# Batch 0's v in four-token runs, w_in in two halves, and slots 0 to 8 in a written order

## The chip, the cores and the metric

The kernel runs on one core of a Trainium2 chip. The metric is the device time of one execution in microseconds (us), from the runtime's own clock; the median of three runs is given, and beside it one execution taken with the hardware profiler. The core's engines are TensorE (PE, matrix multiplies; PEld is its weight load), VectorE (DVE), ScalarE (ACT), GpSimd (POOL) and SyncE (SP). Each works through its own list of instructions in order and waits on semaphores for the others. DMAs are asked for on three of these lists: SP's, ACT's and POOL's.

## The reference

Two stages in one kernel: sliding-window attention with ALiBi bias, then a two-matrix feed-forward block with a hard-swish.

```python
# q, k, v: (8 batches, 8 heads, 576 tokens, 64), float32
scores = scale * q @ k^T                       # scale = 1/8
bias   = slope[h] * -|i - j|,  slope[h] = 2^-(h+1)
mask   = 0 <= i - j < 128                      # causal, window of 128 tokens
attn   = softmax(where(mask, scores + bias, -1e9))
x      = (attn @ v) as 4608 tokens x 512       # heads side by side
h      = x @ w_in                              # w_in: 512 x 2048
out    = (h * clip(h + 3, 0, 6) / 6) @ w_out   # w_out: 2048 x 512, out float32
```

## The kernel before, in words

A **slot** g is one batch and one pair of heads: g = 4 * batch + pair, 32 slots in all. For each slot q and k have to stand with the 64 head dimensions on partitions (`qTb`, `kTb`), the scores are made in PSUM, ScalarE takes the exponential into `pd` (the diagonal 128x128 blocks) and `po` (the blocks below), and the values are multiplied with `v`, to which a column of ones is appended (`vbuf`, 65 wide), so that the row sums come out beside the values. They are divided (`avs`), transposed back, and copied into `xT`, a ring of four batches with d_model on partitions.

The feed-forward part works on blocks nt of 512 tokens. `moe_up(nt, ms)` is one of 16 steps, four 128x512 matmuls with `w_in_sb` into a PSUM bank, then one ACT instruction (`r`, L520) and one DVE instruction (`gbuf`, L521). `moe_down(nt, step)` is four matmuls with `w_out_sb` (L551) of one of four row blocks of 128 tokens; after four of them the bank is copied (L560) and sent out. The list `units` holds all of these steps in order, and `fill(n)` puts the next n of them behind whatever was just issued. So attention's latencies are to be covered with feed-forward steps.

The order is written by hand (`manual_schedule` for all five engines): `first_batch()`, `second_batch()`, then `segment()` for slots 8 to 31. What matters for the change:

- **Batch 0.** q and k come with nine consecutive tokens in each partition (`load_run`), are cast (`prepare`, L208), transposed on TensorE in 64x64 pieces (`transposes`, L219) and copied to `qTb`/`kTb` (L220). For batches 0 and 1 the bias and the mask of the off blocks, for batch 0 also that of the diagonal blocks, are added by TensorE from a table (`tables_diag` L271, `tables_off` L307/L310). v comes token by token (`load_tokens`, L112): each of 128 partitions is one token and receives one 256-byte piece per head, five DMAs for a batch.
- **Slots share space.** `pd` and `po` of slots 0 to 3 lie in `w_out_sb` (`rooms`), those of slots 4 to 7 in `gbuf[1]`. So w_out cannot be loaded before batch 0's values are done. PSUM has two big tiles (`ps_sc`, two banks each, for scores, wide transposes and batch values) and four single banks (two "h", one "av", one "o").
- **Weights.** w_in is loaded on POOL's list with a cast to bf16 in four quarters of 512 columns (`load_w_in`, L166), so that a quarter serves four of the 16 up-steps; the asks stand between POOL's casts. w_out comes in four quarters of 512 rows (`load_w_out`, L171), all asked for in `second_batch` behind slot 6.
- **Later batches.** q and k of batches 1 and 2 come with `load_double` (L98), are cast on POOL (`prepare_double`, L227), transposed (`wide_double` L254, nine 128x128 transposes; `double` L242 in parts of five and four) and copied. From batch 3 on they are transposed by DMA. Slots 8 and up mask their blocks on POOL after the exponential (L405, L414).

## Time and profile before

| what | us |
|---|---|
| median of three runs (322.14 to 323.13) | 322.87 |
| the profiled execution, its own time | 323.39 |
| its span, first to last instruction | 321.4 |
| PE busy, share of the span | 309.9, 96% |
| ACT busy | 195.8, 61% |
| DVE busy | 173.6, 54% |
| POOL busy | 140.2, 44% |
| first up-step on PE starts | 21.3 |
| last w_in quarter landed | 40.5 |
| first down-step on PE starts | 53.8 |
| last w_out quarter landed | 59.8 |

All times inside the execution count from the span's start. "Busy" of PE counts a matmul from its start to its modelled end, and matmuls overlap, so the busy share hides the small pauses; the start times of neighbouring matmuls show them. The granted TensorE clock is 1.0 from beginning to end (0.99 in the last 22 us).

### The profile page before, as it was taken

Reading aid. Unit: us, or ns where it says so; the run is one execution under the profiler, and the core shown is the slowest. Engines: PE = TensorE matmul, PEld = TensorE weight load, DVE = VectorE, ACT = ScalarE, POOL = GpSimd, SP = SyncE. Lnnn points to the kernel's source line nnn. Section 1 sums busy time; section 2 is a strip of 40 time slices with the busy share of each in tenths; the row PEclk is TensorE's granted clock in tenths of the full one; section 3 lists DMA queues with packets and bytes.
Section 4 is the critical chain, followed back from the end, with each engine's and each line's share of the span. In section 5 each row is a group of like instructions: output and inputs, shape, how many; then the busy total and the mean of one; then the engine's idle time right before and its main releaser. Section 6 shows DMA issues by size and latency. Waiting matters only on the chain.

```text
span 321.4 us, 7126 instructions
## 1 busy us (share of the span) xinstructions
PE 309.9 (96%) x2776; PEld 164.8 (51%) x2776; DVE 173.6 (54%) x338; ACT 195.8 (61%) x334; POOL 140.2 (44%) x249
## 2 busy tenths in 40 slices
PE   7879898999999999999999999999999999999996
PEld 6555455454554454444677654444444444444443
DVE  6757565664445555655565546554655455455510
ACT  4748876877777766766676667666764344244401
POOL 7455295586393866276645662763331000000000
PEclk9999999999999999999999999999999999999999
DMA  7999999999999999999999999942212200000112
GB/s 269 205 319 200 233 274 185 234 241 210 201 248 169 217 198 217 196 222 216 208 202 203 228 182 191 246 78 86 23 55 66 73 34 35 33 33 35 65 53 77
DMA packets 131425, 51.90 MB, mean 161 GB/s; under 512 B 118976, under 2 KB 123328, under 8 KB 131392
## 3 DMA queue, kind: packets, MB, share of 16 engines
q1 hardware_dynamic: 126160, 45.36, 66.4%
q0 software_dynamic: 4224, 4.19, 8.4%
q10 hardware_dynamic: 1008, 1.90, 1.6%
q8 instruction: 21, 0.34, 0.5%
q14 instruction: 12, 0.10, 0.1%
HBM read 36.70 MB, written 9.44 MB: 144 GB/s over the span
## 4 chain that ended last, share of the span: by engine, by line
PE 84%; DMA 7%; SPq 3%; POOL 2%; ACT 1%; issue 1%; DVE 1%; ACTq 0%; POOLq 0%
PE ops L551 38%; PE hps L501 36%; DMA ldbuf<-in_q_dram 3%; PE sce L364 3%; PE av L441 2%; DMA w_in_sb<-in_moe_w_in_dram 2%; SPq L112 2%; PE av L433 2%; DMA ldbuf<-in_k_dram 2%; SPq L98 1%; PE ops L532 1%; POOL w_out_sb L171 1%; PE tp L242 1%; POOL pr L227 1%; ACT r L520 0%
## 5 line engine op out<-in xcount | busy, mean ns | idle before, releaser
L521 DVE SCALAR_TENSOR_TENSOR gbuf<-r,hps 128x512 bf16<-128x512 f32 x144 | 98.8, 687 | 102.2 <-ACT r L520 100.9
L520 ACT ACTIVATE r<-hps,bias 128x512 f32<-128x512 f32 x144 | 98.9, 689 | 88.6 <-PE hps L501 88.3
L501 PE MATMUL hps<-xT,w_in_sb 128*128 128x512 bf16 (+1 forms) x640 | 144.9, 358 | 1.7 <-DMA w_in_sb<-in_moe_w_in_dram 1.5
L551 PE MATMUL ops<-w_out_sb,gbuf 128*128 128x512 bf16 x560 | 137.9, 380 | 0.0
L501 PEld LDWEIGHTS <-w_in_sb 128*128 128x128 bf16 x640 | 59.1, 98 | 56.7 <-DMA w_in_sb<-in_moe_w_in_dram 2.3
L551 PEld LDWEIGHTS <-gbuf 128*128 128x128 bf16 x560 | 51.8, 98 | 56.4
L414 POOL TENSOR_SCALAR_AFFINE_SELECT po<-po 128x512 bf16<-128x512 bf16 x48 | 30.2, 633 | 32.7 <-ACT po L412 32.5
L405 POOL TENSOR_SCALAR_AFFINE_SELECT pd<-pd 128x512 bf16<-128x512 bf16 x48 | 29.6, 631 | 31.6 <-ACT pd L388 31.6
L388 ACT ACTIVATE pd<-sce,bias_d 128x512 bf16<-128x512 f32 x48 | 31.6, 683 | 5.4 <-PE sce L372 5.4
L194 POOL CAST tbuf<-ldbuf 128x512 bf16<-128x512 f32 (+1 forms) x45 | 25.5, 611 | 18.6 <-DMA qTb<-tbuf 9.4
L560 DVE COPY osb<-ops 128x512 f32<-128x512 f32 x33 | 22.7, 688 | 20.0 <-PE ops L551 19.9
L412 ACT ACTIVATE po<-sce,bias_o 128x512 bf16<-128x512 f32 x48 | 32.9, 686 | 0.0
L452 DVE TENSOR_TENSOR avs<-av,rc 128x384 bf16<-128x384 f32 (+1 forms) x48 | 23.6, 491 | 1.6
L441 PEld LDWEIGHTS <-pd 128*128 128x128 bf16 x192 | 14.3, 97 | 8.3 <-POOL tbuf L194 0.5
L433 PE MATMUL av<-vbuf,po 128*128 128x65 bf16 x192 | 18.0, 193 | 0.0
L441 PE MATMUL av<-vbuf,pd 128*128 128x65 bf16 x192 | 17.3, 194 | 0.3 <-ACT kTb L244 0.3
L187 POOL CAST vbuf<-ldbuf 128x1024 bf16<-128x1024 f32 x14 | 14.2, 1041 | 5.4 <-DMA ldbuf<-in_v_dram 5.4
L433 PEld LDWEIGHTS <-po 128*128 128x128 bf16 x192 | 14.3, 98 | 2.9 <-DVE avs L452 0.5
L227 POOL CAST pr<-ldbuf 128x576 bf16<-128x576 f32 x20 | 12.8, 668 | 6.0 <-DMA ldbuf<-in_k_dram 3.8
L417 ACT ACTIVATE p4buf<-sce,bias_d 128x64 bf16<-128x64 f32 x48 | 15.4, 321 | 0.0
L364 PE MATMUL sce<-qTb,kTb 64*64 64x192 bf16 (+1 forms) x368 | 11.9, 246 | 0.0
L364 PEld LDWEIGHTS <-kTb 64*64 64x64 bf16 x368 | 7.1, 106 | 8.6 <-issue 8.5
(104 smaller groups left out, 207.8 us busy)
## 6 DMA issues: line engine op xcount, KB each, us to landing
out_dram<-osb SPq DMA_DIRECT2D x33, 256.0 KB, 2.4
ldbuf<-in_v_dram SPq DMA_DIRECT2D x32, 256.0 KB, 5.1
ldbuf<-in_q_dram SPq DMA_DIRECT2D x20, 256.0 KB, 4.8
ldbuf<-in_k_dram SPq DMA_DIRECT2D x16, 256.0 KB, 4.5
ldbuf<-in_q_dram SPq DMA_DIRECT2D x12, 288.0 KB, 7.5
ldbuf<-in_k_dram SPq DMA_DIRECT2D x12, 288.0 KB, 7.8
w_in_sb<-in_moe_w_in_dram POOLq DMA_DIRECT2D x4, 512.0 KB, 9.6
w_out_sb<-in_moe_w_out_dram POOLq DMA_DIRECT2D x4, 512.0 KB, 10.2
```

What stands on the lines that cost most here:

```text
L194: nc.gpsimd.tensor_copy(out=tbuf[:m, :, j, :], in_=s[:m, j, :, :].rearrange("p (i e) d -> p i (e d)", e=2))
L364: nc.tensor.matmul(sce[e][lo:lo + 64, j, :, :].rearrange("p s c -> p (s c)")[:, ds(lo, n)], lhsT=kT[r, j, lo:lo + 64], rhs=qT[r, ds(128 * ...
L388: nc.scalar.activation(out=pd[:, e, :, :], in_=st["sce"][e][:, :, 0, :], func=ACT.Exp, bias=bias_d[:, h:h + 1], scale=scale)
L405: nc.gpsimd.affine_select(out=pd[:, e, :, :], in_=pd[:, e, :, :], pattern=[[0, 4], [1, 128]], channel_multiplier=-1, base=0, compare_op=AL ...
L412: nc.scalar.activation(out=po[:, e, :, :], in_=sc[:, :, 1, :], func=ACT.Exp, bias=bias_o[:, h:h + 1], scale=scale)
L414: nc.gpsimd.affine_select(out=po[:, e, :, :], in_=po[:, e, :, :], pattern=[[0, 4], [-1, 128]], channel_multiplier=1, base=-1, compare_op=A ...
L433: nc.tensor.matmul(out_av, lhsT=po[:, e, qt % 4 if full(g) else qt - 1, :], rhs=vb[:, qt - 1, h, :], start=True, stop=False)
L441: nc.tensor.matmul(out_av, lhsT=d, rhs=vb[:, qt, h, :], start=(qt == 0), stop=True)
L501: nc.tensor.matmul(hps[:, lo:hi], lhsT=w_in_sb[:, ks, ts(ms, 128)], rhs=xT[:, ks, ds(src, hi - lo)], start=(ks == 0), stop=(ks == n_ks - 1))
L520: nc.scalar.activation(out=r6, in_=hps, func=ACT.Relu, bias=bias3[:, 0:1], scale=1.0 / 6.0)
L521: nc.vector.scalar_tensor_tensor(out=gts[nt][:, ms, :], in0=r6, scalar=1.0, in1=hps, op0=ALU.min, op1=ALU.mult)
L551: nc.tensor.matmul(ops[nt, sub], lhsT=gts[nt][:, ms, ts(sub, 128)], rhs=w_out_sb[:, ms, :], start=(ms == 0), stop=(ms == n_ms - 1))
```

## The change

The functions `first_batch` and `second_batch`, with `prepare` and `transposes`, go. In their place a text, `PLAN`, lists one step per line, and `run_plan` calls a function for each; the functions do what the old ones did, cut into single pieces, so that casts, transposes, copies, scores, exponentials, masks, values, and up- and down-steps can stand in any order. `segment` now begins at slot 20 instead of 8. From the scores of slot 13 on, TensorE's instructions follow in the same order as before.

- **v of batch 0** is loaded as four-token runs: partition p of 128 holds tokens 4p to 4p+3 of four heads, in pieces of 1024 bytes (`ldv`, two DMAs), and the last 64 tokens as before (`ldl`). Two casts (`cr`) put them into `tbuf`. TensorE then sorts them (`vp`, `unshuffle`): a 0/1 matrix `sel`, made on VectorE (`sel`: a memset, a reduce, a copy), picks for each block j of 128 tokens the rows 32j to 32j+31, once for each of the four tokens t, summed in PSUM. That is 16 matmuls with 32 rows and 512 columns, two blocks side by side in two banks, and four copies to `vbuf` (`ve`).
- **w_in** comes in two halves of 1024 columns (`wp 0`, `wp 1`) on POOL's list. Both stand behind the casts of batch 1's first k and q.
- **w_out**'s four quarters (`wout`) stand on POOL's list behind the casts of batch 2's q and k of the first double pair.
- **Order.** Batch 0's values are formed in pieces (`vf`, `vr`, `vl`) into a part of `gbuf[0]` (`avs0`). Scores of slots 5 and 4 and all four transposes of batch 1 (`dt 1 ...`) stand ahead of the first up-step, which is now step 6 (`u 0 6`). The up-steps then run in a mixed order: 6, 0, 4, 3, 5, 7, 14, 2, 9, 12, 13, 11, 1, 15, 8, 10.
- **Slots 8 and 9** use the split scores (diagonal and off tiles apart) as slots 4 to 7 do, without tables, with the masks on POOL (`QF = 10`). `p4buf` has four instead of two.
- Some casts and copies change engine: five of batch 2's and 3's k and q casts go from POOL to ACT, two of batch 1's to DVE; one of batch 0's transposed q goes from DVE to ACT.

Counted over the whole program: 16 matmuls with `sel` more, 3 warm-up matmuls fewer (27 for 30), 4 score matmuls fewer net; POOL 9 casts and 2 DMA asks fewer.

```diff
-    def second_w_in():
-        nc.gpsimd.memset(w_out_sb[:, 4, 0:1], 0.0)
-        load_w_in(1)
...
     def scores(g):
-        if full(g):
+        if g < QF:
             scores_diag(g)
             scores_off(g)
             return
...
+    def s_sel():
+        nc.vector.memset(sel, 0.0)
+        diag = sel.rearrange("p (t c) -> p t c", t=4)[:, :, 0:128:4]
+        nc.vector.tensor_reduce(out=diag[:, 0, :], in_=ident.rearrange("p (j i) -> p i j", j=4),
+                                op=ALU.max, axis=mybir.AxisListType.X)
+        nc.vector.tensor_copy(out=diag[:, 1:4, :],
+                              in_=diag[:, 0:1, :].to_broadcast([128, 3, 32]))
...
+    def s_ldv(b, h, n):
+        nc.sync.dma_start(out=vsource(b)[0][:, ds(h, n), :],
+                          in_=v[b, ds(h, n), 0:512, :].rearrange("h (p t) d -> p h (t d)", t=4))
...
+    def s_cr(b, h, n, eng):
+        C[eng](out=vruns[:, :, ds(h, n), :].rearrange("p t h d -> p h t d"),
+               in_=vsource(b)[0][:, ds(h, n), :].rearrange("p h (t d) -> p h t d", t=4))
+
+    def unshuffle(b, h, n, j0, banks):
+        for t in range(4):
+            for i, ps in enumerate(banks):
+                r = slice(32 * (j0 + i), 32 * (j0 + i) + 32)
+                nc.tensor.matmul(ps, lhsT=SEL[r, t, 0:128], rhs=vruns[r, t, ds(h, n), :],
+                                 start=(t == 0), stop=(t == 3))
...
+    def s_wp(i, k0, n):
+        nc.gpsimd.dma_start(out=w_in_sb[:, ds(k0, n), ts(i, 1024)],
+                            in_=moe_w_in[ds(k0 * 128, n * 128), ts(i, 1024)].rearrange(
+                                "(k p) f -> p k f", p=128))
...
-    def first_batch():
-        prepare(0, (V, A))
-        warm_up(20)
...
-    def second_batch():
...
+    def run_plan(text):
+        for line in text.split("\n"):
+            if line.strip():
+                name, *args = line.split()
+                STEPS[name](*(int(a) if a.isdigit() else a for a in args))
...
-        load_tokens(0, "v")
         constants()
         memsets()
-        memsets_later()
-        first_batch()
-        second_batch()
-        fill(2)
-        segment(2 * NP, G, lambda g: FILLS.get(g, (1, 1, 1, 2, 0, 1, 2)))
+        run_plan(PLAN)
+        done[0] = 20 - 1
+        segment(20, G, lambda g: FILLS.get(g, (1, 1, 1, 2, 0, 1, 2)))
```

The plan's first part, up to the first down-step; each step is a line of its own in the kernel and is separated by a semicolon here. V, A and P name the engine of a copy (DVE, ACT, POOL); h, av, o and sc name PSUM banks. `c0` casts a run of batch 0, `t0` transposes it, `e0` copies it out; `td`/`sd` and `to`/`so` are tables and scores of the diagonal and off tiles; `xt`, `xd`, `xo` the exponentials, `md` a mask; `ldd`, `ldt` loads of q or k and of tokens; `pd`, `dt`, `de` cast, transposes and copy of a double pair; `vf`, `vr`, `vl`, `at` values and `nf`, `nr`, `nl`, `na` their division; `bf`, `br`, `bk` transposes back and `ef`, `er`, `ek` copies to `xT`; `vt` casts v; `u`, `ur`, `um` an up-step's PE, ACT and DVE parts, `ub` a begun one; `d` a down-step.

```
c0 1 k A; wu 20; sel; td 0; to 0; c0 0 k V; ldv 0 0 4; mem 7; c0 1 q P; wu 7; c0 0 q V; t0 0 q h; t0 0 k o; t0 1 k h; mem 3;
ldv 0 4 4; t0 1 q av; e0 0 k A; e0 0 q V; sd 0; xt 0; so 0; ldt 1 v 4; td 1; ldd 1 0 q 0; e0 1 q V; e0 1 k A; sd 1; c0 2 k P;
xo 0; ldl 0; xt 1; t0 2 k av; c0 3 k P; t0 3 k h; c0 2 q V; td 2; cr 0 0 4 P; ldd 1 0 k 0; t0 2 q h; e0 2 q A; to 2; e0 2 k V;
sd 2; so 2; pd 1 0 q 0 P; e0 3 k V; mem 6; ldd 1 0 k 1; cr 0 4 4 V; vp 0 0 h av; ve 0 0 8 0 1 V; ve 0 0 8 1 1 V; c0 3 q A;
t0 3 q h; pd 1 0 k 0 P; ldd 1 0 q 1; xt 2; xo 2; e0 3 q V; gl 2 0 P; to 1; so 1; xo 1; vp 0 2 h av; ve 0 0 8 2 1 A; td 3; sd 3;
cl 0 V; to 3; xt 3; so 3; xo 3; pd 1 0 q 1 P; vf 2 h; wp 0 0 4; pd 1 0 k 1 V; dt 1 0 k 0 9 sc; nf 2; ldt 1 v 2; ve 0 0 8 3 1 V;
dt 1 0 q 0 9 sc; de 1 0 k 0 9 A; mem 2; de 1 0 q 0 9 V; ldd 1 1 q 1; vl 3; vf 1 o; vr 0 2 4 h; sd 5; nl 3; xd 5 1; to 5; nf 1;
ldd 1 1 k 1; nr 0 2 4; wp 1 0 4; vr 0 3 3 av; nr 0 3 3; vr 2 2 4 h; nr 2 2 4; ldd 1 1 q 0; pd 1 1 q 0 P; pd 1 1 q 1 P; so 5;
xd 5 0; xo 5; vf 0 h; nf 0; md 5 0; vt 1 4; mem 4; bf 1 av; sd 4; xd 4 1; ef 1 0 512 V; ldd 1 1 k 0; pd 1 1 k 0 V; ldd 2 1 k 0;
ldt 1 v 1; xd 4 0; to 4; so 4; xo 4; bf 3 h; ef 3 0 256 V; pd 1 1 k 1 P; br o; bf 2 h; ef 3 256 256 A; bf 0 av; md 5 1; ldt 1 v 3;
dt 1 1 q 0 9 sc; ef 2 0 512 V; ef 0 0 512 A; de 1 1 q 0 9 V; mem 1; dt 1 1 k 0 9 sc; de 1 1 k 0 9 V; u 0 6 av; ur 0 6; um 0 6;
md 4 1; u 0 0 h; ur 0 0; um 0 0; er A; u 0 4 h; md 4 0; sd 6; xd 6 1; ur 0 4; um 0 4; xd 6 0; ldt 1 v 0; sd 7; u 0 3 o; xd 7 0;
u 0 5 h; xd 7 1; ur 0 5; um 0 5; u 0 7 av; ldt 2 v 3; ur 0 7; um 0 7; ldd 2 0 k 0; ur 0 3; to 7; to 6; um 0 3; vt 1 2; vt 1 0;
mem 0; u 0 14 h; ur 0 14; ldd 2 0 q 1; um 0 14; ldd 2 1 q 0; u 0 2 h; ur 0 2; so 7; xo 7; ldd 2 0 k 1; md 6 0; so 6; u 0 9 o;
ur 0 9; ldt 2 v 2; um 0 2; u 0 12 h; ur 0 12; ldt 3 q 0; u 0 13 av; md 7 1; um 0 9; xo 6; pd 2 0 k 0 P; at 5; md 6 1; ldd 2 0 q 0;
um 0 12; na 5; ldt 2 v 0; pd 2 1 q 0 P; pd 2 0 k 1 P; ldt 2 v 1; md 7 0; ur 0 13; um 0 13; u 0 11 h; at 4; ur 0 11; bk 5 o;
...
pd 2 0 q 0 P; pd 2 0 q 1 P; dt 2 0 q 0 9 sc; um 0 15; de 2 0 q 0 9 A; ek 6 V; ub 1 0 3 o; na 7; ldd 2 1 q 1; bk 7 sc; u 0 10 h;
pd 2 1 q 1 A; ek 7 V; u 1 4 h; u 1 0 o; ur 0 10; um 0 8; wout 1; um 0 10; ur 1 0; ur 1 4; dt 2 1 q 0 5 av; de 2 1 q 0 5 V; sd 8;
xd 8 0; sd 9; wout 0; vt 2 2; u 1 7 h; mem 5; xd 9 1; um 1 0; um 1 4; ur 1 7; u 1 6 av; um 1 7; xd 8 1; u 1 9 h; xd 9 0; ur 1 9;
ur 1 6; ct 3 q 0; vt 2 0; wout 2; um 1 9; u 1 2 o; wout 3; md 8 0; um 1 6; u 1 10 h; ur 1 10; um 1 10; so 8; so 9; ur 1 2; xf 8 1;
u 1 5 h; um 1 2; u 1 8 av; ldd 2 1 k 1; ur 1 8; xf 8 0; x4 8 0; x4 8 1; um 1 8; u 1 3 h; m4 8; ur 1 5; d 0 1 0 o; d 0 1 1 o; um 1 5;
pd 2 1 k 0 P; d 0 0 0 av; xf 9 0; mf 8 0; d 0 0 1 av; ldd 3 1 k 0; d 0 0 2 av; pd 2 1 k 1 A; ur 1 3; um 1 3; ldt 3 q 3; ...
```

## The prediction

> **What bounds the kernel now.** I read the stretches first, cut at two places. By 26.7 us TensorE has done as much useful work as the changed order puts ahead of its first up-step; at 91.1 us stand the last values of slot 11, and from the scores of slot 13 just behind them both orders are the same on TensorE.
>
> ```profile
> 0.00:26.70 26.70, 21.48 (x399) 15.39 (x400) 17.78 (x52) 14.89 (x19) 15.06 (x35) 1.00 1.02 262
> 26.70:91.10 64.40, 61.47 (x604) 32.59 (x601) 36.06 (x62) 51.08 (x86) 38.62 (x63) 1.00 1.08 222
> 91.10:321.40 230.30, 226.97 (x1778) 116.78 (x1777) 119.77 (x224) 129.86 (x230) 86.50 (x153) 1.00 0.66 133
> ```
>
> Behind the length stand PE, PEld, DVE, ACT, POOL, the granted clock and the DMA engines' share. In the last stretch TensorE is busy 227.0 of 230.3 us, some 3 of the rest being the last output: TensorE is the bound, and its list there is not changed. The change is worth what it does to the arrival at the second cut. Ahead of that cut the DMA engines never rest (1.02, 1.08). Next TensorE's waits, then its timeline:
>
> ```profile
> PE hps L501 <- DMA w_in_sb<-in_moe_w_in_dram: 1.5, 3, 0.8
> PE tp L242 <- POOL pr L227: 1.0, 1, 1.0
> PE tp L254 <- POOL pr L227: 0.9, 1, 0.9
> ```
> ```profile
> 28.80 1.04 PE L501 MATMUL hps<-xT,w_in_sb 128*128 128x512 bf16 x4 [0.49 <-DMA w_in_sb<-in_moe_w_in_dram]
> 35.83 1.04 PE L501 MATMUL hps<-xT,w_in_sb 128*128 128x512 bf16 x4 [0.81 <-DMA w_in_sb<-in_moe_w_in_dram]
> ...
> 49.05 0.45 PE L242 MATMUL tp<-ident,pr 128*128 128x128 bf16 x5 [1.00 <-POOL pr L227]
> ...
> 54.66 1.03 PE L501 MATMUL hps<-xT,w_in_sb 128*128 128x512 bf16 x4
> 55.52 0.44 PE L242 MATMUL tp<-ident,pr 128*128 128x128 bf16 x5
> ```
>
> The waits are short and many. The last two rows price an up-step: 55.52 - 54.66 = 0.86 us. The other engines' timelines show why the waits are there:
>
> ```profile
> 7.32 1.02 ACT L395 ACTIVATE w_out_sb<-scd 128x1024 bf16<-128x1024 f32 x1 [0.49 <-PE scd L296]
> 8.39 1.02 ACT L376 ACTIVATE w_out_sb<-sco 128x1024 bf16<-128x1024 f32 x1
> ```
> ```profile
> 28.52 1.48 POOL L166 DMA_DIRECT2D w_in_sb<-in_moe_w_in_dram  x2
> 43.55 2.99 POOL L171 DMA_DIRECT2D w_out_sb<-in_moe_w_out_dram  x4
> 47.70 2.50 POOL L227 CAST pr<-ldbuf 128x576 bf16<-128x576 f32 x4
> ```
>
> Batch 0 is a ping-pong of scores and exponentials; w_in's last two quarters are asked for at 28.5 us and landed at 35.8 and 40.5; the four w_out asks (2.99 us of POOL) hold up the casts that TensorE waits 1.00 us for at 49.05.
>
> **The work ahead of the first up-step, after.** TensorE, by differences of start times: four times 36 small transposes at 0.79 (3.2); 8 diagonal tables at 0.215 (1.7); six off tables at 0.44 (2.6); scores of six slots, a pair of 64-row matmuls in 0.055 (3.0); values of four slots at 0.53 (2.1); 20 transposes back and 36 of batch 1 at 0.055 (3.1); the unshuffle. Its 32-row matmuls are not in the trace. Bounds: alone, 16 x 0.215 = 3.4; two at a time, as the 64-row score pairs run, 1.7. I take 1.7, the row nearest in form: different rows of the array, different banks. Sum 17.4 us, the warm-up apart. Before, the same work less the unshuffle was done at 26.7 us.
>
> **When it is done (T).** ACT's list ahead of it: ten exponentials of 1024 at 0.92 from start to start (9.2), five copies or casts of 576 (2.8), four exponentials of 512 at 0.59 (2.4), one copy of 1152 (1.0), three smaller ones (1.4): 16.8. It starts with slot 1's k, landed at 6.3, so T is at least 23.1. In the batch 0 of before ACT worked 8.5 of 12.5 us; at that share T is 31.0. I go through the steps between. `sel` (three small DVE instructions, some 0.5) stands ahead of slot 0's casts, which begin at 5.2 and not 4.7; the first transposes start at 6.2 (before 5.4), slot 0's scores at 7.7 (6.9). Each further table needs one of two score tiles, released by an exponential. The unshuffle wants both v casts: the last q, k land at 9.6, then 1.0 MB in 1024-byte pieces, between 2.6 us (q, k rate, 0.74 per 288 KB) and 4.2 (v rate, 1.0 per 256 KB); I take 2.7, 1024 bytes being nearer to q's 2304 than to 256. So v is there at 12.3, the cast at 12.9, the two unshuffles at 13.2 and 15.6, each with its copies in front of the next scores. Last exponential of batch 0 ends 19.1; batch 1's first k copied 20.1; slot 3's values divided 21.9 (its tile is then slot 5's off table); slot 5's off exponential 24.1; slot 4's 26.6; copy of slot 0 into `xT` 27.4. T = 27.5, 0.8 later than before. DVE's list to there adds to 19.0 from 4.6, which makes 23.6: it is not the bound, but close.
>
> **w_in.** The ask waits for the cast of batch 1's q: behind v on SP's queue come two small loads (1.0) and four of 0.74, landed 16.3; cast 0.67; asked 17.0, where quarter one was asked for at 12.4. w_out's quarters landed 3.3 apart, so a half takes 6.6; about 3 us of loads on SP's queue run beside it: first half 27, just hidden. The second stands behind it on the same queue: 34. TensorE wants it for up-step 14, behind six up-steps (5.2), two score groups (0.5) and two tables (0.9): 34.1. I count 0.5 for it. On SP a load of batch 2's k waits for DVE's cast of batch 1's last k (26); queued behind it are three tiles of batch 1's v. I take it that they land by 36.5, behind w_in, and POOL's casts of them end at 37.7; the values of slot 5 want them at 39.1: 1.4 us of cover.
>
> **What goes and stays from T to the second cut.** 57.4 us of work took 64.4 before. Pauses over 0.15 us add to 4.4: two for w_in (1.6), the casts and the mask chain around 45 to 50 us (1.7), and four of 0.2 to 0.3 later. They go with the order; the other 2.6 are switches between matmul forms and stay. New pauses: between none and 4.4 again; I take 1.2, the 0.5 for w_in and 0.7 where an up-step waits for a bank (ACT's seven instructions between 30 and 35 us make it late with step 3, whose bank step 9 wants at 36.2).
>
> **At nothing:** w_out, asked for from 44.4 on, landed near 49, 52, 56 and 59 at 3.3 each, wanted from 57.5 to 61.8: cover 2 to 5 us, and without it 0.9 per step that waits. Slots 8 and 9 in split form (18 matmuls for 10 or 23, about 0.5 us each way). Five casts more on ACT (2.9) against five `xT` copies fewer (2.7), in a stretch where it is busy 51.1 of 64.4. SP's load for batch 3 that waits for a POOL cast near 58 holds batch 3's q and batch 2's last v tile, wanted at 68, landed 63.
>
> **Sum.** +0.8 (T) - 4.4 + 1.2 = -2.4 us. The profiled execution's own time is 323.39 (span 321.4 and 2.0 around it): 321.0. It lies 0.5 above the median of 322.87, so 320.5 for the median.
>
> **Rivals.** *The second half of w_in is late (slower).* For it: the last two quarters of before needed 12 us from ask to landing beside SP's loads; at that pace both halves need 24, land at 41.0, and TensorE stands 6.9 us at up-step 14 where I count 0.5: 326.9. It decides from a landing at 37.0 on (34.1 + 0.5 + 2.4), where the gain is gone. Against it: those 12 us were shared with v's 256-byte tiles, and w_out's quarters passed by such tiles:
>
> ```profile
> 50.26 10.56 SPq L112 DMA_DIRECT2D ldbuf<-in_v_dram  x5
> ```
>
> The first of these, asked for at 50.3, landed at 60.1, right behind the last of w_out at 59.8. The Trainium skill, "DMA: Bandwidth & Descriptors", section "Queues, rings and completion order", has each DMA engine take turns between queues packet by packet; by that rule w_in would share evenly with batch 2's q and k, whose pieces are nearly as long, and by an estimate from the 6.6 above, doubled for the second half, land near 40.2 and give 326.1. The v row agrees with turns by packet, since small pieces then get little; no row here has w_in beside q and k alone.
>
> *Nothing gained.* The unshuffle does not pair (+1.7) and the small pauses come back in part (+0.7): 322.9. For it: no 32-row row; two unshuffles on the chain. *All gained.* ACT waits half as long as I walked (T 25.5) and no new pause: 320.5 - 2.0 - 1.2 = 317.3. For it: ACT's floor of 23.1; against it: DVE's 23.6 alone.
>
> **Chances.** As forecast 0.42, all gained 0.17, nothing gained 0.15, late half 0.26. 0.3% is 1.0 us, about what a measurement can tell. Faster: 0.39 + 0.17 + 0.03 = 0.59; same: 0.03 + 0.10 = 0.13; slower: 0.02 + 0.26 = 0.28. The likeliest alone: 319.3 to 321.8. The range reaches to the two ends, the upper cut within the late half: 317.5 to 325.8.
>
> **What would show it.** Right: first up-step at 26 to 29, up-step 14 with a wait under 1 us, slot 13's scores near 89 instead of 91.5, the rest of equal length. Unshuffle: 16 matmuls starting within 1.8 us in all, or 3.5. Wrong: a long row "hps <- DMA w_in_sb" after 34; ACT or DVE gaps that put T beyond 30; a down-step waiting for w_out; or a last stretch longer than 230 us because the earlier arrival meets loads that are not there.

## The result and the profile after

The changed kernel takes 326.25 us (median of 14 executions, 322.96 to 328.33) where the kernel before takes 322.73 (14 executions, 320.99 to 323.29). The ratio is 1.0105, with a 95% interval of 1.0082 to 1.0128. So the change is 1% slower; I had forecast 320.5, and 325.8 as the upper end of the range.

The times come in two groups that go with the granted TensorE clock: of the 14 executions five have a mean clock of 0.999 or 1.0 and take 322.96 to 325.15 us, nine have 0.983 to 0.990 and take 325.94 to 328.33. Of the 116 executions of the kernel before that were taken beside the experiments below, three have less than 0.998 (0.994, 0.995 and 0.995). The profiled execution of the changed kernel is one at 1.0; its own time is 325.15 (before 323.39). Ratios here and below leave out an execution that is disturbed beyond that, such as the one of 328.33.

These are its stretches, cut where the first up-step and slot 13's scores stand (columns as before):

```profile
0.00:29.80 29.80, 23.55 (x456) 17.08 (x456) 20.68 (x65) 18.88 (x25) 16.21 (x37) 1.00 1.00 266
29.80:91.70 61.90, 58.97 (x552) 32.69 (x561) 37.32 (x66) 48.87 (x85) 30.86 (x50) 1.00 1.09 223
91.70:323.40 231.70, 224.30 (x1744) 116.81 (x1769) 119.28 (x223) 130.27 (x231) 87.00 (x153) 1.00 0.63 130
```

The kernel before, cut at the same work, reads:

```profile
21.34:91.47 70.13, 66.30 (x651) 35.70 (x651) 39.06 (x67) 53.66 (x90) 42.18 (x69) 1.00 1.08 228
91.47:321.40 229.93, 226.62 (x1772) 116.48 (x1769) 119.44 (x224) 129.86 (x230) 86.13 (x152) 1.00 0.65 133
```

Slot 13's scores come at 91.70 and not near 89; they are 0.23 later than before, and the first up-step is at 29.80 and not 27.5. The last stretch is 1.8 us longer. The list of TensorE's waits has none for w_in and none for w_out. In its timeline the unshuffle, the first up-step and the longest waits are:

```profile
14.84 1.04 PE L900 MATMUL bank<-tbuf,sel 32*128 32x512 bf16 x8 [1.40 <-DVE tbuf L893]
17.08 1.18 PE L900 MATMUL bank<-tbuf,sel 32*128 32x512 bf16 x8
...
29.80 2.75 PE L459 MATMUL bank<-xT,w_in_sb 128*128 128x512 bf16 x11
...
74.09 0.66 PE L783 MATMUL bank<-ident,pr 128*128 128x128 bf16 x9 [1.09 <-POOL pd L663]
...
91.35 0.20 PE L391 MATMUL av<-vbuf,po 128*128 128x65 bf16 x1 [1.17 <-DVE avs L959]
...
148.71 0.52 PE L347 MATMUL sce<-qTb,kTb 64*64 64x192 bf16 x16 [1.12 <-DMA kTb<-tbuf]
```

The unshuffle pairs (8 matmuls in about 1 us), but TensorE stands 1.40 us ahead of it, for v. The wait at 148.71, a transposed k that is late, is what makes this execution's last stretch long. It is not in the next profiled execution of the same kernel (first experiment), whose last stretch, from slot 13's scores to the last matmul, takes 226.7 us as before (226.8). So the change does not bring it every time. The waits at 74.09 and 91.35 come back in e1, e2, e4, e5, e6 and e8 (1.2 to 1.6 us and 1.2 us). For the first, SyncE's and GpSimd's timelines show the cause:

```profile
46.98 15.93 SPq L677 DMA_DIRECT2D ldbuf<-in_k_dram  x2
62.95 2.71 SPq L684 DMA_DIRECT2D ldbuf<-in_q_dram  x3
...
67.64 1.86 SPq L677 DMA_DIRECT2D ldbuf<-in_k_dram  x3
```
```profile
61.44 0.29 POOL L944 TENSOR_SCALAR_AFFINE_SELECT p4buf<-p4buf 128x128 bf16<-128x128 bf16 x1 [6.84 <-ACT p4buf L938]
61.68 0.66 POOL L774 CAST pr<-ldbuf 128x576 bf16<-128x576 f32 x1
...
72.54 0.67 POOL L774 CAST pr<-ldbuf 128x576 bf16<-128x576 f32 x1 [0.24 <-DMA ldbuf<-in_k_dram]
```

The second of the two k loads in the first SyncE row waits until 62.4 for the cast at 61.68 to free its buffer; GpSimd does that cast only behind a mask for which it stands 6.84 us. Nine loads stand behind it on SyncE's queue. The seventh and eighth are the two blocks of batch 3's k that TensorE wants next, at 72.8: they land at 72.4 and 73.2, and their casts end at 73.2 on GpSimd and at 74.0 on ScalarE. (The wait is put down to the mask on GpSimd that ends near then; it has nothing to do with it.)

### The profile page after: what moved, and what is told of

It reads as the page before. It is cut to its first block, busy times and chain, and to the rows that moved or that the text cites. A ratio compares the mean times of both kernels' runs of the same rounds, so it can differ in the third digit from the quotient of the medians.

```text
span 323.4 us, 7079 instructions
## 1 busy us (share of the span) xinstructions
PE 306.8 (95%) x2747; PEld 166.6 (52%) x2785; DVE 177.3 (55%) x353; ACT 198.0 (61%) x340; POOL 134.1 (41%) x239
## 4 chain that ended last, share of the span: by engine, by line
PE 74%; DMA 10%; issue 5%; POOL 4%; ACT 2%; DVE 2%; SPq 2%; POOLq 0%
PE ops L509 24%; PE hps L459 22%; PE bank L459 9%; PE bank L818 6%; DMA ldbuf<-in_v_dram 3%; DMA ldbuf<-in_k_dram 2%; PE sce L347 2%; DMA qTb<-tbuf 2%; DMA kTb<-tbuf 2%; PE av L399 2%; PE av L391 1%; SPq L684 1%; PE ops L490 1%; DMA xT<-avs 1%; POOL w_out_sb L175 1%
## 5 line engine op out<-in xcount | busy, mean ns | idle before, releaser
L478 ACT ACTIVATE r<-hps,bias 128x512 f32<-128x512 f32 x83 | 57.1, 688 | 64.5 <-PE hps L459 63.5
L479 DVE SCALAR_TENSOR_TENSOR gbuf<-r,hps 128x512 bf16<-128x512 f32 x83 | 57.1, 688 | 60.4 <-ACT r L478 59.5
L509 PE MATMUL ops<-w_out_sb,gbuf 128*128 128x512 bf16 x354 | 87.5, 379 | 1.5 <-issue 1.0
L459 PE MATMUL hps<-xT,w_in_sb 128*128 128x512 bf16 (+1 forms) x390 | 82.5, 344 | 0.2
L811 DVE SCALAR_TENSOR_TENSOR gbuf<-r,bank 128x512 bf16<-128x512 f32 x61 | 41.4, 686 | 36.3 <-ACT r L806 35.8
L459 PE MATMUL bank<-xT,w_in_sb 128*128 128x512 bf16 x236 | 59.5, 379 | 0.7
L806 ACT ACTIVATE r<-bank,bias 128x512 f32<-128x512 f32 x61 | 41.6, 692 | 20.0 <-PE bank L459 18.9
L818 PE MATMUL bank<-w_out_sb,gbuf 128*128 128x512 bf16 x171 | 42.3, 379 | 1.1 <-issue 1.0
L658 ACT ACTIVATE pd<-sce,bias_d 128x512 bf16<-128x512 f32 x44 | 28.8, 684 | 6.4 <-PE sce L355 3.7
L518 DVE COPY osb<-ops 128x512 f32<-128x512 f32 x21 | 14.4, 688 | 17.3 <-PE ops L509 17.3
```

The lines of the kernel that those rows point to most:

```text
L459: nc.tensor.matmul(hps[:, lo:hi], lhsT=w_in_sb[:, ks, ts(ms, 128)], rhs=xT[:, ks, ds(src, hi - lo)], start=(ks == 0), stop=(ks == n_ks - 1))
L478: nc.scalar.activation(out=r6, in_=hps, func=ACT.Relu, bias=bias3[:, 0:1], scale=1.0 / 6.0)
L479: nc.vector.scalar_tensor_tensor(out=gts[nt][:, ms, :], in0=r6, scalar=1.0, in1=hps, op0=ALU.min, op1=ALU.mult)
L509: nc.tensor.matmul(ops[nt, sub], lhsT=gts[nt][:, ms, ts(sub, 128)], rhs=w_out_sb[:, ms, :], start=(ms == 0), stop=(ms == n_ms - 1))
L806: nc.scalar.activation(out=r6, in_=st["u", nt, ms][0], func=ACT.Relu, bias=bias3[:, 0:1], scale=1.0 / 6.0)
L811: nc.vector.scalar_tensor_tensor(out=gts[nt][:, ms, :], in0=st["r", nt, ms], scalar=1.0, in1=st["u", nt, ms][0], op0=ALU.min, op1=ALU.mult)
```

## The experiments

In all of them (e1 to e15) the last stretch, from slot 13's scores to the last matmul, was 226.6 to 227.7 us. What differs is when slot 13's scores come, and the clock. "First up-step" and "slot 13" are of the profiled execution; the last column counts executions with a mean clock below 0.997. A **filler** is a useless matmul that only keeps TensorE busy: `warm 6 o` is six of them with 512 columns.

| kernel | median us (before beside it) | ratio, 95% | first up-step | slot 13 | low clock |
|---|---|---|---|---|---|
| changed, as given | 326.25 (322.73) | 1.0105, 1.0082 to 1.0128 | 29.80 | 91.70 | 9 of 14 |
| e1 changed again | 324.37 (322.43) | 1.0108, 1.0069 to 1.0147 | 29.57 | 91.86 | 3 of 7 |
| e2 three fillers | 326.65 (322.43) | 1.0132, 1.0113 to 1.0152 | 32.27 | 94.35 | 0 of 4 |
| e3 before, less warm-up | 322.25 (322.43) | 0.9996, 0.9979 to 1.0014 | 21.19 | 90.33 | 0 of 12 |
| e4 v by token | 325.86 (322.43) | 1.0120, 1.0099 to 1.0141 | 32.16 | 94.31 | 6 of 6 |
| e5 two fillers | 323.91 (322.03) | 1.0058, 1.0034 to 1.0081 | 29.45 | 91.31 | 1 of 12 |
| e6 one filler | 324.02 (322.03) | 1.0056, 1.0034 to 1.0077 | 29.91 | 91.97 | 0 of 12 |
| e7 late pauses filled | 323.91 (322.03) | 1.0059, 1.0035 to 1.0083 | 29.58 | 91.00 | 0 of 12 |
| e8 first 20 us reordered | 323.49 (322.03) | 1.0047, 1.0022 to 1.0072 | 28.94 | 91.82 | 1 of 12 |
| e9 cast early | 322.10 (322.29) | 1.0003, 0.9982 to 1.0024 | 29.47 | 90.14 | 0 of 12 |
| e10 cast and 90 us | 322.09 (322.29) | 0.9998, 0.9977 to 1.0019 | 29.73 | 89.82 | 0 of 12 |
| e11 all of these | 322.62 (322.29) | 1.0013, 0.9995 to 1.0032 | 29.01 | 90.38 | 0 of 12 |
| e12 slots 10 to 13 | 321.53 (321.96) | 0.9996, 0.9968 to 1.0024 | 29.72 | 89.28 | 1 of 12 |
| e13 best | 321.60 (321.96) | 0.9980, 0.9961 to 0.9999 | 28.97 | 89.58 | 2 of 12 |
| e14 v by token, clean | 324.85 (321.96) | 1.0088, 1.0062 to 1.0114 | 31.68 | 93.74 | 1 of 6 |
| e15 w_out earlier | 327.22 (322.12) | 1.0144, 1.0109 to 1.0178 | 29.20 | 93.91 | 5 of 6 |

My theory on reading the result was twofold: a lower clock in most executions, because TensorE has too little to do in the first 15 us, and a later first up-step. The rival was that the clock is chance and the time lost is lateness alone.

### e1 to e3: the clock

e1 is the changed kernel untouched.

> The changed kernel once more, untouched, as the yardstick of the next three runs. Theory (clock): its times fall into two groups, near 324 us at a mean granted clock of 0.999 or more and near 326.5 us at 0.983 to 0.990, about two runs in three in the second group; the runs of before stay at 0.999 or more. Rival (chance of the hour or of the chip): before shows the low clock as often, and the difference of the two kernels is that of their profiled executions, 1.8 us.

Four executions at 0.999 or 1.0 take 323.61 to 324.37 us, three at 0.990 take 326.82 to 327.62. Over both takings the changed kernel has 12 of 21 executions at 0.990 or less, with a median of 326.78, and nine at 0.999 or 1.0, with a median of 323.98: the low clock costs 2.8 us, and the kernel is still 1.5 us behind where it does not occur. The kernel before shows it in 3 of 116, so the rival falls.

e2:

```diff
-wu 7
+wu 25
 so 0
+warm 4 o
...
+warm 6 o
 vp 0 0 h av
```

> The changed kernel with useless matmuls where TensorE stood still in its first 15 us: 18 warm-ups more at 5.1 us, four of 512 columns behind slot 0's off scores, six ahead of the first unshuffle (their bank is free). Theory (clock): TensorE's first stretches are too short and the granted clock is raised later in most runs; with the holes filled every run has 0.999 or more, and the median goes from 326 to 324 us. Rival (lateness alone): the holes do not matter, clock and time stay as in the untouched kernel, or the time rises by up to 0.5 us where a filler overruns its hole.

The clock held in all four (0.998 to 1.0), as the theory had it; the time did not fall, because the early filler overran: in this execution the clock was raised only at 7.43 us (4.42 in e1), the added warm-up matmuls ran at half rate, and the first up-step came at 32.27.

e3, the kernel before:

```diff
         tables_off(0)
-        warm_up(10)
         transposes(0, (V, A))
```

> The kernel before with 20 warm-up matmuls where it has 30: TensorE's first busy stretch ends near 5.6 us where it ended at 6.15. Theory (clock): granted clock of 0.983 to 0.990 turns up in a good part of the runs and the median rises by 1 to 2.5 us. Rival: ten matmuls of 0.055 us beside nothing else change nothing, 322.7 us at 1.0.

No effect, 0.9996, and no low clock in 12 executions. The theory was wrong here: ten warm-up matmuls fewer do not bring the low clock into this kernel.

### e5 and e6: which hole

e5 is e2 without the first edit; e6 has the last edit alone, six fillers ahead of `vp 0 0 h av`.

> The changed kernel with useless matmuls in the two later holes only: four of 512 columns behind slot 0's off scores (8.4 to 9.4 us) and six ahead of the first unshuffle (13.2 to 14.6); the early warm-up stays at 7. Theory (clock): the three fillers together held the clock at 0.998 or more in all four runs, and their loss of time came from the early one alone, which overran (first up-step at 32.0 and not 29.5). So here the clock stays up in every run, the first up-step is at 29.3 to 29.8, and the median is that of the untouched kernel's runs at full clock: 323.5 to 324.5 us. Rival (the early filler did it): the low clock comes back in half of the runs, median 325.5 or more.

> Only the six filler matmuls ahead of the first unshuffle, where TensorE stands still for 1.4 us while v is on its way. If this hole, the longest, is what drops the clock: 0.998 or more in all runs and 323.5 to 324.5 us, as with both. If the holes only act together (little matmul work between 5 and 15 us): the low clock stays in part of the runs and the median lies between 324 and 326.5.

In e5 the clock is up in 11 of 12 executions, and the first up-step is at 29.45: the early filler was what cost e2 its time. In e6, six useless matmuls of 0.215 us in the hole at 13.2 to 14.6 us make the kernel faster: 12 of 12 executions at 0.999 or 1.0, ratio 1.0056 where the untouched kernel has 1.0105. The first up-step did not move. So 1.6 us of the 3.5 us lost (0.0049 of 322, each ratio being good to some 0.002) are the clock, and to fill the 1.4 us in which TensorE waits for v is enough to keep it.

How it falls is in the traces of three later kernels, whose profiled execution was caught by it. e14, with two pauses of 0.8 and 0.9 us between 7 and 10 us, and e15, with one of 3.0 us at 51; stretches cut where the clock record changes:

```profile
6.61:10.02 3.41, 1.76 (x80) 1.56 (x77) 1.88 (x3) 2.24 (x4) 0.82 (x2) 1.00 1.17 326
10.02:13.43 3.41, 3.36 (x48) 1.62 (x47) 1.15 (x2) 2.48 (x3) 1.13 (x2) 0.50 1.20 205
```
```profile
52.22:55.63 3.41, 1.01 (x21) 0.83 (x22) 0.68 (x2) 1.84 (x3) 0.97 (x1) 1.00 1.19 242
55.63:59.04 3.41, 3.35 (x8) 1.16 (x8) 2.62 (x5) 3.29 (x6) 1.24 (x2) 0.50 1.24 206
```

Read the second number (TensorE's busy time) and the clock, third from the end. After 3.41 us with 1.76 or 1.01 us of matmuls, the next 3.41 us run at half clock; in e4, after 0.43 us, it is the next 6.83 us. The profiled executions of the changed kernel and of e1, the same kernel, kept their clock. On the same grid of 3.41 us, begun where the clock was raised, their emptiest stretches are these:

```profile
11.14:14.55 3.41, 2.11 (x44) 1.24 (x42) 1.74 (x3) 3.14 (x5) 0.99 (x1) 1.00 1.16 225
```
```profile
72.69:76.10 3.41, 1.84 (x24) 1.32 (x25) 1.37 (x2) 2.98 (x6) 2.66 (x5) 1.00 1.18 300
```

So 1.84 us were enough where 1.76 were not. (The second row is the pause at 72 us; e6 still has that one, without a low clock.) Slid along the matmul records around the wait for v, a stretch of that length is emptiest with 1.82 us in the changed kernel (from 11.45 on) and 1.95 in e1 (from 11.25); the kernel before has nothing below 2.15. That is near the edge, but in neither execution beyond it. So where the grid happens to lie does not by itself explain a drop in 12 of 21 executions, and no trace of the untouched kernel caught one. A mean clock of 0.989 over 325 us is 7.1 us at half, about two steps of the grid as in e4, where e14 and e15 show one. What is shown is that filling this hole keeps the clock; how it drops in the untouched kernel stays open. The Trainium skill, "TensorE: Matmul & The Clock Gate", Part 1, has a free-running window of 3.4 us, half and full as the only clocks, and a return to half after an idle window; length and values agree with the rows, but the window need not be idle: 1.76 us of work in it did not keep the clock.

### e4 and e14: v token by token

```diff
-sel
...
-ldv 0 0 4
+ldt 0 v 0
+ldt 0 v 1
...
-cr 0 4 4 V
-vp 0 0 h av
-ve 0 0 8 0 1 V
-ve 0 0 8 1 1 V
+cv 0 1 V
+cv 0 2 V
```

(likewise for the other half). e14 has this, 14 fillers in the hole that it opens, and the earlier cast of e9 (below).

> The changed kernel with v of batch 0 loaded token by token as before (five loads of 256-byte pieces at the places of the new loads, five plain casts in place of sorting casts, unshuffle and copies; the selection matrix is left out too). Prediction's pricing: v lands 1.0 us per tile, so near 14.7 and not at 14.0, TensorE saves the unshuffle (1.7 us of its list) and slot 0's casts begin 0.9 us earlier, so the first up-step comes 0 to 1.5 us earlier than 29.8 and the time is 323 to 326. Rival (the runs of v were needed to keep the later order fed): v's last tile lands near 16, batch 1's loads behind it are 2 us late, w_in is asked for near 21, and the first up-step comes after 31: 327 to 329.

> v of batch 0 token by token in the changed order, with 14 filler matmuls in the 3.6 us hole where TensorE waits for v, and the cast early as in the others. If the hole alone dropped the clock there, it stays at 0.998 or more. Theory: v's tiles, and batch 1's loads behind them, land 2 us later than in runs; without the slow clock the first up-step comes near 31 (32.2 with it), 1 to 1.5 us behind the run with the moved cast, 323.1 to 323.6. Rival (the unshuffle costs what the loads gain): 322.0 to 322.5.

In e4 v's tiles land at 10.5 to 15.9 us. Batch 1's loads behind them come later than in the changed kernel (the second half of its first k at 20.13 and not at 18.12), and w_in is asked for at 21.6 and not at 19.6. TensorE stands 3.48 us, but not for v: it wants VectorE's cast of that k, which ends at 20.97 (the row names the instruction behind it). The clock falls to half behind this hole, from 20.63 to 27.46.

```profile
21.12 2.08 PE L783 MATMUL wide<-ident,pr 128*128 128x128 bf16 x18 [3.48 <-DVE rcn L698]
```

The first up-step comes after 31, as the rival had it, but the time of 325.86 lies in the theory's range, and the ratio of 1.0120 cannot be told from the changed kernel's 1.0105. So e4 decides nothing. In e14 the clock held in five of six executions (the sixth dropped it at 10.02, behind the pauses shown above). Its first up-step is at 31.68, 2.2 us behind e9, and the time 324.85 against 322.10. But the fillers overran their hole. TensorE, VectorE and GpSimd:

```profile
19.70 2.97 PE L631 MATMUL bank<-tab,ident 128*128 128x512 bf16 x13
22.51 1.17 PE L783 MATMUL wide<-ident,pr 128*128 128x128 bf16 x18
```
```profile
19.60 0.75 DVE L774 CAST pr<-ldbuf 128x576 bf16<-128x576 f32 x1 [1.81 <-POOL ldbuf L688]
```
```profile
20.56 0.66 POOL L774 CAST pr<-ldbuf 128x576 bf16<-128x576 f32 x1 [0.95 <-DMA ldbuf<-in_q_dram]
```

The last cast of k was done at 20.35 and that of q at 21.22, and the transposes of both began only at 22.51, when the fillers were through. A down-step also waits 1.23 us for w_out at 67.95, which none does in e9. By an estimate from these rows, nine transposes could have begun near 20.5 and the other nine near 21.4, VectorE's copy of q behind them near 22.1 where it stands at 23.71, and the first up-step would be near 30.0, 0.5 us behind e9. The times of the theory and of its rival, that the unshuffle costs what the loads gain, were both missed, neither is settled, and what v in four-token runs is worth stays open.

### e7 and e8: the late pauses, the first 20 us

e7 moves work into the pauses (on top of e5): `d 0 2 1 h` and `d 0 2 2 h` ahead of `dt 3 0 k 0 5 av`, `u 1 13 o` ahead of `va 9 0 3`, `d 1 0 3 h` between `va 11 0 3` and `va 11 3 2`.

> The two fillers, and two places of the written order changed so that TensorE has work in the pauses at 72 us (1.25 to 1.8 us, batch 3's k prepared late) and at 90 us (1.34 us, the second half of slot 11's values waits for the bank of the first): two down-steps go ahead of the transposes of batch 3's k, one up-step behind them, and the last down-step of tile 1, sub-tile 0 goes between the two halves of slot 11's values. Theory (the pauses lie on the chain, since TensorE is the bound behind them): 2.2 to 2.8 us less than with the fillers alone, so 321.0 to 322.0, the second cut near 88.5. Rival (what follows waits for loads in any case): the gain is taken back by waits for the transposed k or q of batches 4 and 5, and the time falls by less than 1 us.

The rival's number held, though not its reason: slot 13 came 0.3 us earlier, the time did not change. Filling a pause with the next work only moves it when what follows is late for reasons of its own: there are new waits of 0.56 and 0.79 us for VectorE's products of the up-steps that had been brought forward, and of 0.7 us for slot 12's exponentials.

e8 (of the fillers it has only the four behind slot 0's off scores; the third copy of unshuffled v also goes from ScalarE to VectorE):

```diff
-sel
...
 so 0
+warm 4 o
...
 c0 2 q V
+sel
...
-vp 0 0 h av
-ve 0 0 8 0 1 V
-ve 0 0 8 1 1 V
 c0 3 q A
...
 xo 1
-vp 0 2 h av
-ve 0 0 8 2 1 A
+vp 0 0 h av
+ve 0 0 8 0 1 V
+ve 0 0 8 1 1 V
 td 3
 sd 3
 cl 0 V
+vp 0 2 h av
+ve 0 0 8 2 1 V
 to 3
```

> The first filler, and the first 20 us in another order: the selection matrix is built on VectorE behind slot 2's q cast and not ahead of slot 0's casts, and the first unshuffle stands behind slot 3's q and slot 1's off scores and not ahead of them. Theory (the late arrival of v, 13.97 and not 12.3 as I took it, and the 0.9 us of selection matrix put the first up-step at 29.5 where I had 27.5): last exponential of batch 0 ends near 19 and not 21, first up-step 27.3 to 28.3, time 1.2 to 2.2 us less than with the fillers alone, so 322 to 322.8. Rival (ACT's and VectorE's lists behind set the first up-step): it moves by less than 0.7 us and the time stays at 323.5 or more.

The first up-step is at 28.94, 0.5 us earlier and not 1.2 or more, so the rival held, and even the 0.5 was lost at 70 us, where slot 8's values now waited 0.9 us for batch 2's last v tile: it too stands in the late queue of loads.

### e9 and e10: the cast that holds the loads

e9 is e6 with one GpSimd cast moved:

```diff
 md 8 0
+pd 2 1 k 0 P
...
 m4 8
...
-pd 2 1 k 0 P
```

> The one filler of the run before, and on GpSimd the cast of batch 2's last k block goes from behind the mask of slot 8's last block (which GpSimd stands 6.8 us for, from 54.3 to 61.1) to ahead of it. SyncE's load of batch 3's k, which waits 18 us for that cast (44.5 to 62.6), and the nine loads queued behind it then go out near 55. Theory (that queue is why batch 3's k is late at 72 us): the DMA engines no longer fall to 3 GB/s near 62 us, the pause of 1.25 to 1.8 us at 72 is gone, slot 13's scores come 1.0 to 1.4 us earlier than 91.97, and the median falls from 324.0 to 322.6 to 323.0. Rival A (the loads now run beside w_out's quarters and make them late): a down-step waits near 58 to 63, and the time is 324 or more. Rival B (the slots' own exponentials set the pace behind 70 us): the pause goes, but the time comes back at 75 to 93 us, and the median stays within 0.4 us of 324.0.

The time is 322.10, level with the kernel before. From e6 to e9 the medians fall by 1.9 us and the ratios, each against the kernel before on the same chip, by 0.0053 or 1.7 us. GpSimd and SyncE in e9:

```profile
54.23 0.65 POOL L774 CAST pr<-ldbuf 128x576 bf16<-128x576 f32 x1
61.11 0.29 POOL L944 TENSOR_SCALAR_AFFINE_SELECT p4buf<-p4buf 128x128 bf16<-128x128 bf16 x1 [6.23 <-ACT p4buf L938]
```
```profile
44.44 11.00 SPq L677 DMA_DIRECT2D ldbuf<-in_k_dram  x2
55.49 6.62 SPq L684 DMA_DIRECT2D ldbuf<-in_q_dram  x3
```

and the stretch around 62 us, of e6 and then of e9 (last two numbers: the DMA engines' share and GB/s):

```profile
60.50:63.00 2.50, 2.50 (x13) 1.15 (x12) 1.38 (x2) 2.50 (x6) 1.45 (x3) 1.00 0.17 25
```
```profile
60.50:63.00 2.50, 2.50 (x13) 1.14 (x12) 0.97 (x2) 2.50 (x7) 1.89 (x4) 1.00 1.19 257
```

In e6 the DMA engines had all but stood still with loads waiting to be asked for. Batch 3's two blocks of k now land at 69.8 and 70.7, the wait at 72 us is gone, and slot 13's scores come at 90.14 (91.97 in e6, which differs in this instruction alone). w_out's last quarter landed at 62.7: rival A did not happen, rival B fell too.

e10 adds `d 1 0 3 h` between the two halves of slot 11's values.

> The same, and the last down-step of tile 1, sub-tile 0 between the two halves of slot 11's values, where TensorE waits 1.34 us for the bank near 90 us. Theory (as with the moved cast): of the 1.34 us, the run with both late pauses filled kept 0.4, because slot 13's scores then wait for slot 12's exponentials; so 0.3 to 0.5 us below the run with the moved cast alone. Rival: all 1.2 us are gained, since the earlier loads let slot 12 begin earlier too.

Slot 13's scores come 0.3 us earlier, the time does not change (322.09), and neither the theory nor the rival held; the wait moved to slot 13's scores, which want slot 12's exponentials:

```profile
90.60 0.49 PE L347 MATMUL sce<-qTb,kTb 64*64 64x192 bf16 x15 [0.54 <-ACT p4buf L938]
```

### e11 to e13 and e15: how far it goes

e11 joins e8 (with its one filler), e9 and e10. e12 is e10 with `d 1 0 2 h` behind `sq 12` too and w_out's last two quarters asked for right behind the first two. e13 is e11 with these edits, `so 3` and `xo 3` ahead of `vp 0 2 h av`, the cast `pd 1 0 k 1` ahead of `ve 0 0 8 2 1`, and the transposes `dt 1 0 k 0` ahead of `vf 2 h`.

> Everything together: first filler, selection matrix and first unshuffle later, cast early, down-step between the halves. Theory (first up-step 0.5 us earlier as measured, which so far was lost at 70 us because batch 2's last v tile stood in the same late queue of loads): gains add up, 0.5 us below the run before this, so near 321.8 to 322.4 and level with the kernel before or just below it. Rival: no gain over the run before this, the first 30 us being without effect on what follows.

> The run with the moved cast and the down-step between the halves, and two more: a second down-step of the same tile goes from ahead of slot 12's scores to behind them, and w_out's last two quarters are asked for right behind its first two. Theory (slot 13's scores wait for slot 12's exponentials, which began 0.86 us too late): slot 12's scores come 0.8 us earlier, the waits of 1.3 us near 89 to 91 us go, the time falls by 0.8 to 1.2 us to 320.9 to 321.3. Rival (slot 12's scores are themselves held by the exponentials of slot 11): less than 0.3 us.

> All that helped: first filler, selection matrix and first unshuffle later, and now slot 3's off scores ahead of the second unshuffle and batch 1's last k cast ahead of its copy; cast early, w_out's quarters together, the two down-steps behind slot 12's scores. Theory: last exponential of batch 0 ends near 18.7, first up-step 27.8 to 28.4 (1.2 to 1.6 us earlier than in the run with one filler), and the time is 1 us below the run before this: 319.9 to 320.5, under the kernel before. Rival (ScalarE's and VectorE's lists set it): first up-step at 28.8 or later, no gain over the run before this.

e11 is no faster than e10 (its rival held). In e12 slot 12's scores come 0.8 us earlier and slot 13's at 89.28, so part of the wait near 90 us was the order; the median is 321.53, but by the ratio (0.9996 against 0.9998) no gain over e10 is shown. e13 has no gain over e12, and its first up-step is later than 28.8: the rival again.

What sets the first up-step shows when all the traces are laid side by side. In each kernel with the changed order it starts 7.9 to 8.0 us behind VectorE's first copy of batch 1's transposed q (8.92 in e4, whose clock is at half there), and VectorE is busy 7.3 to 7.4 us of that. In the changed kernel two chains meet at the copy. Behind batch 0's last exponential, q's transposes wait for the tile that it releases at 21.10 and are through at 21.81. And on VectorE's own list slot 2's division and a copy of unshuffled v stand ahead, and they end at 21.83.

```profile
21.15 0.66 PE L783 MATMUL wide<-ident,pr 128*128 128x128 bf16 x9 [0.24 <-ACT w_out_sb L359]
```
```profile
21.15 0.68 DVE L916 CAST vbuf<-bank 128x512 bf16<-128x512 f32 x1
21.86 1.36 DVE L787 COPY qTb<-wide 128x1152 bf16<-128x1152 bf16 x1
```

From the end of this exponential to the copy it is 0.74 to 0.76 us here and in e1, e2 and e5 to e12. In e13 the exponential ends at 18.72, 2.4 us earlier, and q's transposes begin at 19.55, yet the copy starts only 0.8 us earlier. The same two steps of VectorE's list stand ahead of it:

```profile
20.45 0.68 DVE L916 CAST vbuf<-bank 128x512 bf16<-128x512 f32 x1
21.05 1.35 DVE L787 COPY qTb<-wide 128x1152 bf16<-128x1152 bf16 x1
```

So it takes both chains to move the first up-step, and with the exponential out of the way VectorE's list holds it. No run tests another order of these two steps and the copy.

Both e11 and e13 lose 0.9 to 1.1 us at 64 us, where w_out's last quarter is now late (it landed at 64.85 in e13):

```profile
64.89 0.81 PE L818 MATMUL bank<-w_out_sb,gbuf 128*128 128x512 bf16 x3 [0.88 <-DMA w_out_sb<-in_moe_w_out_dram]
```

e15 tries to mend that: e13 with w_out's first two quarters asked for behind `md 7 0`, 3 us earlier, and the other two where the first two stood.

> The run with everything, and w_out's first two quarters asked for behind slot 7's last mask (near 44 us) and not behind batch 2's q casts (near 47). Theory: the quarters come one behind the other, 3.1 to 3.7 us each, so the last lands near 62 and no down-step waits; batch 2's k and v are there before 50 in any case; 0.8 to 1.0 us less, 320.6 to 320.8. Rival (the loads of batches 2 and 3 are pushed back by the same 3 us): the wait moves to the values of slot 8 or to batch 3's k near 70 us, and the time stays at 321.6.

It came out as the rival had it, and worse: w_out landed by 60.9, but batch 2's last q and k, asked for as in e13, landed at 53.6 and 55.1 where e13 had 49.1 and 49.8. TensorE stood 3.0 us for the cast of that q, and the clock fell behind it (rows above).

```profile
54.39 0.45 PE L783 MATMUL bank<-ident,pr 128*128 128x128 bf16 x5 [2.97 <-ACT pr L774]
```

The lowest ratio is e13's: 0.998, interval 0.9961 to 0.9999, barely below the kernel before.

## Why the prediction was wrong

**Direction.** I forecast 2.4 us less; it is 3.5 us more. Four steps failed, in the prediction's order:

- *T, the first up-step: 27.5; measured 29.45 to 29.91 in the changed kernel and the seven others that leave the order of its first 30 us alone and do not overrun a hole, so 2.0 to 2.4 late.* The chain that I walked is one of the two that hold T: from batch 0's last exponential to T I had 8.4 us (19.1 to 27.5), and it took 8.7 (21.10 to 29.80). What failed are two durations ahead of that exponential: the selection matrix took 0.96 us of VectorE, not 0.5 (the first transposes at 6.2 hold all the same), and v was there at 13.97, not 12.3: 4.35 us behind the last k, outside even my upper bound of 4.2. So the unshuffles stood at 14.84 and 17.08 where I had 13.2 and 15.6, and the exponential ended 2.0 us late. The rate that I took for v was not what failed: of its 1024 pieces 994 had begun by 11.5 us, and the last 30 straggled in up to 13.2. What held these up was not tested. VectorE's list, "not the bound, but close", is the other: with the exponential 2.4 us earlier in e13, T moved by only 0.8.
- *"At nothing": SyncE's load that waits for a GpSimd cast.* The prediction names this wait, with its place and the loads behind it, and passes it for free because the last v tile of batch 2 lands at 63, before it is wanted. But the cast came at 61.7 and not near 58, that tile landed at 70.5, and batch 3's k behind it, which I had not followed, at 72.4 and 73.2. Measured: a pause of 1.1 to 1.6 us at 72, and 1.7 us in e9 for moving the cast. This term was in view.
- *The late pauses: 0.7 us allowed for banks; the one near 90 us alone took 1.3.* Here `va 11 3 2` follows `va 11 0 3` with nothing between and one bank for both. From the first up-step to the second cut I had 61.2 us; it took 61.6. That is luck: the two pauses alone took 2.6 us, from start to start, where I had 1.2 for all, and the rest 59.0 where I had kept 60.0. With the cast moved it took about 60.4.
- *The granted clock: 1.00 in every row I read, and not a term of the sum.* It cost 1.6 us (e6). The walk itself had placed the wait for v (v at 12.3, unshuffle at 13.2), and how little TensorE has to do around it was not looked at.

What held: the unshuffle pairs (eight matmuls in 1.0 us and eight in 1.1, 2.1 in all, where I had 1.7 paired and 3.4 not); w_in asked for at 19.6 landed at 28.6 and 34.3, where I had 27 and 34, and up-step 14 did not wait, so the rival of the late half fell; no down-step of the changed kernel waited for w_out, but by luck: its quarters landed at 55.7 to 63.7 and not at 49 to 59, the first down-step came at 60.4 and not at 57.5, and e11 and e13 did wait; the last stretch is of equal length to about 1 us in every kernel but for the one late transpose. The change is slower, the side on which the late half of w_in would have put it, but by other mechanisms.

Together: clock 1.6 and cast 1.7, by the ratios, make up what was lost against the kernel before but for 0.1 us (e9: 1.0003). In the profiled execution of the changed kernel, which kept its clock, the second cut came at 91.4 where the sum gives 88.7: 2.3 of the 2.7 us are T, 0.4 the stretch behind it. That T is also what separates e9 from the forecast is argued: a later T cost most of its lateness (e2 against e5: 2.8 us in T, 2.4 in the time by the ratios), but an earlier one, by 0.5 to 0.8 us in e8, e11 and e13, gained nothing that is clear of the noise, since a v tile or w_out was then waited for.

## What to carry to other kernels

When an order written out by hand is changed, follow each queue to its last entry: the instruction that waits costs nothing by itself, the eighth load behind it does, and the DMA engines' rate over short stretches shows it sooner than any wait of TensorE (25 GB/s around 62 us in e6, where the mean from 30 to 92 us in the changed kernel is 223). Look in the new order for the emptiest few microseconds of TensorE and fill them, with useless matmuls if need be: six of them were worth 1.6 us here. But see that a filler ends before the hole does (e2, e14). A pause filled with the next work, or a transfer asked for earlier, is gained only if nothing else is late behind it (e7, e10, e15).

## What the runs showed of the hardware that I had not expected

- TensorE's clock dropped to half for 3.41 us after a stretch of 3.41 us with 1.76 us of matmul work (e14), and did not after one with 1.84 us (e1). In a kernel of 324 us a low clock cost 2.8 us, in 12 of 21 executions of the same program.
- 1.0 MB of v in 1024-byte pieces, queued behind q and k, was complete 4.35 us after the last k (9.62 to 13.97), though 994 of its 1024 pieces had begun by 11.5.
- With w_out's first two quarters asked for 3 us earlier, q and k tiles of another queue, asked for at the same times to 0.2 us, landed 4.5 and 5.3 us later (e13 to e15). The Trainium skill, "DMA: Bandwidth & Descriptors", section "Queues, rings and completion order", has each DMA engine take turns between queues packet by packet. That the work of one queue delays another agrees with it; the turns themselves these rows do not show.
